# Chunk-selected attention with a LayerNorm-MLP behind it: the gain folded into W1, less work on VectorE, and a new order

## The chip, the core and the metric

One core of one Trainium2 chip runs the whole kernel in one launch. The metric is the device time in microseconds (us), lower is better. TensorE (PE in the rows) multiplies, VectorE (DVE), ScalarE (ACT) and GpSimd (POOL) work on elements, SyncE (SP) only issues DMAs, and sixteen DMA engines move the data. Each engine takes its instructions strictly in the order in which they were written for it.

## What is computed

Attention over 4 batches, 8 heads, 768 positions and 64 dimensions, in which a query sees only the 6 key chunks (of 32 keys) with the highest upper bound, then LayerNorm, a two-layer MLP and a residual sum:

```python
k_min, k_max = k_chunks.min(axis=3), k_chunks.max(axis=3)            # 24 chunks of 32 keys
ub = np.sum(np.maximum(q * k_min, q * k_max), axis=-1)               # per query and chunk
ub = np.where(causal, ub, -1e9)                                      # only chunks up to the query's own
top_chunks = np.argsort(ub, axis=-1)[..., -6:]
scores = np.where(sel & (i >= j), q @ k.T / 8, -1e9)
x = softmax(scores) @ v                                              # heads side by side: 512 wide
xn = (x - mean(x)) / np.sqrt(var(x) + 1e-6) * g_ln
out = x + np.maximum(xn @ w_ch1, 0) @ w_ch2                          # 512 -> 2048 -> 512
```

## The kernel before, in words

Two heads share the 128 partitions: a group g (0 to 15) is one pair of heads of one batch, `b, hp = divmod(g, 4)`. The 768 positions are 6 tiles of 128. Tile 0 of every batch needs no selection and is done by the functions that end in `a` (`lda`, `turna`, `smma`, `sexpa`, `valuesa`, `norma`). Batch 0's tiles 1 to 5 are loaded by tile, for four pairs at once, and turned on TensorE by the functions that end in `t` (`ldt`, `turnt`, `boundst`, `selectt`, `masktt`). Groups 4 to 15 are loaded by 32-wide blocks (`ldb`) and turned on VectorE (`turn`).

For each group: `kbound` takes minimum and maximum of a chunk's keys (DVE), `kdiag` makes the bound's operand from them (POOL), `qhi`, `qlo`, `qrel` split q into parts of 16 bits (ACT, DVE), `bounds` multiplies them (PE, into PSUM: two halves, `ub[:, :, 0]` and `ub[:, :, 1]`), `select` (DVE) adds the two halves and the causal term, finds the eight largest of each row and writes a mask, `maskt` turns it (PE), `mring` and `qring` put mask and q where the scores' matmul reads them. Then `smm` (PE), `sexp` (ACT), `diag` (POOL), `values` (PE), `norm` (DVE) give x in a range r of tiles (r=0: tiles 1 and 2, r=1: tiles 3 to 5), and `pstat` takes its statistics, one pair at a time.

A unit u is what the MLP works on at once: units 0 and 1 are the tiles 0 of batches 0, 1 and 2, 3; unit 2+2b+r is range r of batch b. `centre` (L621) subtracts the mean and multiplies by g (tile `gall`), one instruction of 512 columns per tile (L629); the result `xc` is turned either on TensorE (`xtp`, L648, copied out by `xtc`; units 0 and 1) or by a transposing DMA on SP's queue (`xt`, L642, L646; the other units). `m1` (L670) multiplies by a quarter of W1, `relu` (L686, ACT) evicts, `m2` (L699) multiplies by W2, `fin` (L708) adds x and stores. W1 and W2 come in four quarters each through POOL's queue (`w1`, `w2`), which turns them to 16 bits.

Nothing schedules this: a hand-written table of names, `ORDER`, is run from front to back, and every engine's instructions are tied to that order:

```python
for one in ORDER.split():
    what, _, way = one.partition("@")
    other[0] = int(way or 0)
    ...
    env[fn](*(int(a) if a.isdigit() else a for a in args))
    for ins in done[n:]:
        if ins.engine in queues:
            if ins.engine in ahead:
                tc.add_manual_dep(ins, ahead[ins.engine], inorder, reason="order")
```

So an instruction that waits holds up all that stands behind it on its engine, on SP's and POOL's DMA queues too. PSUM gives four one-bank buffers (`ps_t`) and two two-bank buffers (`ps_m`).

Of the kernel before, what the change touches and what calls it, by code (L numbers as in the profile page):

```python
# [850 lines left out]
```

## Time and profile before

| | |
|---|---|
| median of 3 runs | 295.56 us (294.69 to 296.43) |
| the profiled execution | 296.29 us, of which the trace's span is 294.6 us |
| PE busy | 263.3 us, 89% of the span |
| DVE busy | 217.8 us, 74% |
| ACT busy | 175.6 us, 60% |
| POOL busy | 109.3 us, 37% |
| mean granted clock of TensorE | 0.954 |
| DMA | 31.52 MB, mean 107 GB/s |

Shares of the whole span mix stages. The page's strip of 40 slices shows three of them: up to about 40 us DVE is full while PE has gaps and a lower clock, then a stretch to 220 us in which PE and DVE are both nearly full (with a hole at 66 to 74 us), then 70 us in which PE alone works without a gap. So the table says where to look for a time, and the rows of the stages say what it is worth.

### The profile page before, as it was taken

The numbers are of one execution on the slowest core, as the hardware profiler recorded it, in microseconds if no ns is written. First come the engines' busy times: TensorE is split into PE (matmuls) and PEld (weight loads), VectorE is DVE, ScalarE is ACT, GpSimd is POOL, SyncE is SP. The second block draws the span as 40 slices with busy tenths as digits, with TensorE's granted clock in tenths as the row PEclk, the third lists the DMA queues.
The fourth block names the chain that finished last, engine by engine and source line by source line (L and its number), as shares of the span: only waits on it lengthen the run. The fifth ranks groups of instructions, "written<-read, shape, count | busy, mean of one in ns | idle before, by whom it ended". The sixth has DMA issues, their size and how long they took to land.

```text
span 294.6 us, 6890 instructions
## 1 busy us (share of the span) xinstructions
PE 263.3 (89%) x2680; PEld 183.5 (62%) x2680; DVE 217.8 (74%) x627; ACT 175.6 (60%) x223; POOL 109.3 (37%) x209
## 2 busy tenths in 40 slices
PE   3658789991999997999899989998999999999995
PEld 3446679870677664666587656766776756775553
DVE  6989999733859899999999999999974238331122
ACT  2735767331489787878578867895666755343320
POOL 8783854500712327842440443445523111010000
PEclk9855799997799999999999999999999999999999
DMA  9999897198948799994889438145922102032012
GB/s 165 218 216 180 110 207 124 32 141 131 108 108 135 144 167 142 174 149 65 130 136 185 88 66 140 27 45 76 87 71 60 38 0 56 17 85 77 36 48 98
DMA packets 127601, 31.52 MB, mean 107 GB/s; under 512 B 118608, under 2 KB 124496, under 8 KB 127568
## 3 DMA queue, kind: packets, MB, share of 16 engines
q1 hardware_dynamic: 93936, 22.43, 39.3%
q0 software_dynamic: 29328, 7.34, 26.3%
q10 hardware_dynamic: 4304, 1.31, 2.4%
q8 instruction: 21, 0.34, 0.5%
q14 instruction: 12, 0.10, 0.1%
HBM read 27.53 MB, written 6.29 MB: 115 GB/s over the span
## 4 chain that ended last, share of the span: by engine, by line
PE 50%; DVE 24%; DMA 10%; SPq 8%; POOL 3%; issue 2%; ACT 2%; DVEq 0%; POOLq 0%
PE mm L670 21%; PE yp L699 17%; SPq L202 6%; PE mm L534 6%; DMA qnb<-in_q_dram 4%; PE sm L568 3%; DVE xc L629 3%; DMA knb<-in_k_dram 2%; DVE ot L708 2%; DVE qnT L405 2%; DVE m L477 1%; DVE q L418 1%; DMA out_dram<-ot 1%; DVE QB L117 1%; DVE knT L405 1%
## 5 line engine op out<-in xcount | busy, mean ns | idle before, releaser
L545 ACT ACTIVATE pt<-mm 128x1024 f16<-128x1024 f32 (+2 forms) x96 | 81.0, 880 | 29.5 <-PE mm L534 28.2
L699 PE MATMUL yp<-w2b,hT 128*128 128x512 f16 (+2 forms) x400 | 93.3, 371 | 0.3 <-DVE ot L708 0.3
L670 PE MATMUL mm<-xT,w1b 128*128 128x256 f16 (+1 forms) x640 | 90.3, 296 | 2.6 <-DMA xT<-xc 1.5
L670 PEld LDWEIGHTS <-w1b 128*128 128x128 f16 x640 | 62.2, 99 | 25.1 <-issue 2.0
L686 ACT ACTIVATE hT<-mm 128x768 f16<-128x768 f32 (+1 forms) x56 | 49.7, 900 | 44.2 <-PE mm L670 40.4
L699 PEld LDWEIGHTS <-hT 128*128 128x128 f16 x400 | 37.2, 98 | 33.4 <-DVE x L582 0.5
L553 POOL TENSOR_SCALAR_AFFINE_SELECT pt<-pt 128x512 f16<-128x512 f16 (+1 forms) x32 | 25.5, 802 | 69.7 <-ACT pt L545 69.6
L708 DVE SCALAR_TENSOR_TENSOR ot<-yp,rstd,x 128x512 f32<-128x512 f32 (+2 forms) x25 | 17.8, 718 | 29.1 <-PE yp L699 23.6
L534 PE MATMUL mm<-QA,KA 128*128 128x128 f16 (+2 forms) x224 | 34.0, 247 | 1.8 <-ACT pt L545 0.6
L534 PE MATMUL mm<-QB,KB 128*128 128x128 f16 (+2 forms) x224 | 33.8, 247 | 0.2
L568 PEld LDWEIGHTS <-pt 128*128 128x128 f16 x640 | 23.6, 98 | 4.2 <-POOL pt L553 0.5
L640 POOL TENSOR_TENSOR rstd<-ve,mhalf 128x2 f32<-128x2 f32 (+1 forms) x10 | 8.3, 828 | 47.1 <-DVE ve L637 43.4
L568 PE MATMUL sm<-va,pt 128*128 128x65 f16 x520 | 24.0, 194 | 0.5 <-ACT pt L545 0.3
L534 PEld LDWEIGHTS <-KA 128*128 128x128 f16 x224 | 18.0, 100 | 10.1 <-issue 0.8
L212 POOL DMA_DIRECT2D va<-in_v_dram x24 | 21.4, 894 | 0.7 <-issue 0.5
L534 PEld LDWEIGHTS <-KB 128*128 128x128 f16 x224 | 18.5, 101 | 4.8 <-issue 1.4
L629 DVE SCALAR_TENSOR_TENSOR xc<-x,mv,gall 128x512 f16<-128x512 f32 x24 | 19.3, 850 | 0.0
L581 DVE RECIPROCAL rden<-sm 128x4 f32<-128x4 f32 (+1 forms) x32 | 5.6, 176 | 17.9 <-PE sm L568 17.9
L619 DVE BATCH_NORM_STATS2 bst<-x 128x6 f32<-128x128 f32 x80 | 17.8, 278 | 0.1
L405 DVE STREAM_TRANSPOSE qnT<-qnb 128x640 f32<-128x640 f32 x12 | 10.0, 831 | 9.9 <-DMA qnb<-in_q_dram 9.9
L415 ACT ACTIVATE q<-qnT 128x640 f16<-128x640 f32 x12 | 8.8, 736 | 13.8 <-DVE qnT L405 13.3
L582 DVE TENSOR_TENSOR x<-sm,rden 128x256 f32<-128x256 f32 (+1 forms) x32 | 15.7, 491 | 1.1
(105 smaller groups left out, 353.8 us busy)
## 6 DMA issues: line engine op xcount, KB each, us to landing
out_dram<-ot SPq DMA_DIRECT2D x23, 256.0 KB, 2.1
qnb<-in_q_dram SPq DMA_DIRECT2D x48, 80.0 KB, 2.8
knb<-in_k_dram SPq DMA_DIRECT2D x48, 80.0 KB, 3.1
w1b<-in_moe_w_ch_dram POOLq DMA_DIRECT2D x4, 512.0 KB, 6.8
w2b<-in_moe_w_ch_dram POOLq DMA_DIRECT2D x4, 512.0 KB, 9.3
va<-in_v_dram POOLq DMA_DIRECT2D x24, 80.0 KB, 3.7
knt<-in_k_dram SPq DMA_DIRECT2D x5, 256.0 KB, 6.4
qnt<-in_q_dram SPq DMA_DIRECT2D x5, 256.0 KB, 7.1
```

The lines of the kernel that those rows point to most:

```text
L212: nc.gpsimd.dma_start(va[:, hh, :, 0:D], v[b, 2 * hp + hh, P:S].rearrange("(t p) d -> p t d", p=P))
L405: nc.vector.transpose(t, st[g][nm].rearrange("p c e -> p (c e)"))
L534: nc.tensor.matmul(sc[:, hh, o:o + w * P], ks[:, (t - 1) * P:t * P] if t else k0, qs[:, (s - 1) * P:(s - 1 + w) * P], start=True, stop=True,)
L545: nc.scalar.activation(st[g]["pt", r][:, 4 * i:4 * i + o].rearrange("p n h x -> p h n x"), st[g]["sc", r, i][:, :, 0:o * P].rearrange("p h ...
L553: nc.gpsimd.affine_select(out=dv, in_=dv, compare_op=ALU.is_ge, fill=0.0, base=0, pattern=[[0, 2 * (z - a)], [1, P]], channel_multiplier=-1,)
L568: nc.tensor.matmul(pv[:, hh, s - a, :], pt[:, where[t, s], hh, :], va0[:, b * H + 2 * hp + hh, 0:D + 1] if t == 0 else sb[t]["va"][:, 2 * ...
L619: nc.vector.bn_stats(half(u)["st"][:, i, hp], flat(xt_(u)[:, i, 2 * hp:2 * hp + 2]))
L629: nc.vector.scalar_tensor_tensor(h["xc"][:, i, :], flat(xt_(u)[:, i]), h["mv"][:, i, 0:1], gall, op0=ALU.subtract, op1=ALU.mult,)
L670: nc.tensor.matmul(hp_[:, i // (per(u) // 2), o:o + w], w1b[:, kt, (m + i) * P:(m + i + 1) * P], h["xT"][:, kt], start=(kt == 0), stop=(kt ...
L686: nc.scalar.activation(o, i, ACTF.Relu, scale=HS)
L699: nc.tensor.matmul(h["yp", i][:, cs], h["hT", kt // 4][:, kt % 4, i * P:(i + 1) * P], w2b[:, kt, cs], start=(kt == 0), stop=(kt == KT2 - 1),)
L708: nc.vector.scalar_tensor_tensor(ot[:, cs], h["yp", i][:, cs], h["rstd"][:, i:i + 1], flat(xt_(u)[:, i])[:, cs], op0=ALU.mult, op1=ALU.add,)
```

## The change

- `gall` (g over all partitions) goes; g is loaded as a column (`gcol`) and multiplied into W1 once, in place, by 16 instructions of `w1g` (DVE, 128x512 f16). `centre` only subtracts the mean, with a TENSOR_SCALAR in the place of the SCALAR_TENSOR_TENSOR.
- `lows`/`lowst` copy one half of the bounds out of PSUM on ACT. `select` then adds the two halves in one instruction for all columns, the causal term in a second one on the 4 columns of each row's own chunks alone, and `max` looks only at columns up to the own chunks.
- `pstat` takes statistics of two pairs at once: 40 instructions of 256 columns, where there were 80 of 128.
- x of unit 2 is turned on TensorE too (`xtp.2`, `xtc.2`), beside units 0 and 1.
- `zeros`, `warm.14` and `busy(n)`: products of a zero tile, 128x256 each, ahead of named PE steps, into the buffer that the step then fills: 14 at the start and 83 further ones, of which all but five stand ahead of the first `m1` in PE's order.
- A new `ORDER`.

The diff, cut to its core:

```diff
-    causf = const.tile([P, NQ, 2, NCH], F32, name="causf", tag="causf")
+    causd = const.tile([P, NC4], F32, name="causd", tag="causd")
-    gall = const.tile([P, DM], F32, name="gall", tag="gall")
+    gcol = const.tile([P, KT1], F32, name="gcol", tag="gcol")
+    zer = const.tile([P, 2 * P], F16, name="zer", tag="zer")
+    def busy(o):
+        for _ in range(other[0]):
+            nc.tensor.matmul(o, zer[:, 0:P], zer, start=True, stop=True)
...
+    def w1g(j):
+        c = slice(j * HID // 4, (j + 1) * HID // 4)
+        eng = pick(nc.vector, nc.gpsimd)
+        for kt in range(KT1):
+            eng.tensor_scalar(w1b[:, kt, c], w1b[:, kt, c], gcol[:, kt:kt + 1], None, op0=ALU.mult)
...
     def turnt(s, nm):
         ps = sb[s][nm + "T"] = ps_t.tile([P, HP, P], F32, name="tr", tag="one")
+        busy(ps[:, 0:2].rearrange("p n x -> p (n x)"))
...
+    def lows(g):
+        st[g]["ubl"] = smp.tile([P, NQ, 2, NCH], F32, name="ubl", tag="ubl", bufs=1)
+        copy(pick(nc.scalar, nc.vector), st[g]["ubl"], st[g]["ub"][:, :, 1])
     def select(g):
-        nc.vector.tensor_tensor(ubt, ub[:, :, 1], causf, ALU.add)
-        nc.vector.tensor_tensor(ubm, ub[:, :, 0], ubt, ALU.add)
+        nc.vector.tensor_tensor(ubm, ub[:, :, 0], st[g]["ubl"], ALU.add)
+        nc.vector.tensor_tensor(own, own, causd.unsqueeze(1).unsqueeze(1).to_broadcast([P, NQ, 2, NC4]), ALU.add)
         for s in range(NQ):
             for hh in range(2):
-                nc.vector.max(m8[:, s, hh, :], ubm[:, s, hh, :])
+                nc.vector.max(m8[:, s, hh, :], ubm[:, s, hh, 0:(s + 2) * NC4])
...
-            nc.vector.bn_stats(half(u)["st"][:, i, hp], flat(xt_(u)[:, i, 2 * hp:2 * hp + 2]))
+            nc.vector.bn_stats(half(u)["st"][:, i, hp // 2], flat(xt_(u)[:, i, 2 * hp - 2:2 * hp + 2]))
...
-            nc.vector.scalar_tensor_tensor(
-                h["xc"][:, i, :], flat(xt_(u)[:, i]), h["mv"][:, i, 0:1], gall, op0=ALU.subtract, op1=ALU.mult,
+            pick(nc.vector, nc.gpsimd).tensor_scalar(
+                h["xc"][:, i, :], flat(xt_(u)[:, i]), h["mv"][:, i, 0:1], None, op0=ALU.subtract,
             )
...
-        ident rows lda.0.kn masks small lda.0.qn rrows.3 turna.0.kn rrows.1 kbounda.0 ldt.1.kn ldt.2.kn ldt.1.qn
...
+        zeros warm.14 rows small ldt.1.kn ldt.2.qn ldt.2.kn ident turnt.1.kn turnt.2.qn qhit.2 lda.0.kn rows0
+        lda.0.qn turnt.2.kn@6 ldva.0 rrows.1 turna.0.kn@6 rrows.0 qlot.2 ldt.1.qn kboundt.1 kdiagt.1 kbounda.0
...
```

What the table does to the engines' queues shows at three places. The first is SP's queue behind the last loads of batch 0 (`knt`, `qnt` are its tiles, `qnb`, `knb` the blocks of groups 4 and on). Before:

```order
L219 DMA knt_754<-in_k_dram 128x8x64
L219 DMA qnt_824<-in_q_dram 128x8x64
L646 DMA_TRANSPOSE xT_922<-xc_869 128x4x128 x2
L202 DMA qnb_1024<-in_q_dram 32x20x32 x4
L202 DMA knb_1031<-in_k_dram 32x20x32 x4
```

And now:

```order
L233 DMA knt_660<-in_k_dram 128x8x64
L233 DMA qnt_1055<-in_q_dram 128x8x64
L216 DMA qnb_1082<-in_q_dram 32x20x32 x4
L216 DMA knb_1087<-in_k_dram 32x20x32 x4
L216 DMA qnb_1255<-in_q_dram 32x20x32 x4
L216 DMA knb_1381<-in_k_dram 32x20x32 x4
L216 DMA qnb_1386<-in_q_dram 32x20x32 x4
L744 DMA out_0_dram<-ot_1399 128x512
```

The two transposing DMAs of unit 2's `xc` no longer stand ahead of the first blocks.

The second is DVE around the centring of unit 0 (`bst`, `mv` are its statistics, `x2_590` and `x2_597` unit 2's x, written as groups finish). Before:

```order
L399 BN_STATS bst_500<-x2_501 128x6 x2
L627 BN_AGGR mv_624<-bst_500 128x2 x2
L629 SCALAR_TENSOR_TENSOR xc_625<-x2_501,mv_624,gall_116 128x512 x2
L581 RECIPROCAL rden_669<-sm_533 128x4
L582 TENSOR_TENSOR x2_590<-sm_533,rden_669 128x2x2x64
```

And now:

```order
L657 BN_AGGR mv_616<-bst_468 128x2 x2
L659 TENSOR_SCALAR xc_617<-x2_469,mv_616 128x512 x2
L611 RECIPROCAL rden_625<-sm_581 128x4
L612 TENSOR_TENSOR x2_597<-sm_581,rden_625 128x2x2x64
L196 TENSOR_SCALAR w1b_114<-w1b_114,gcol_116 128x512 x4
L611 RECIPROCAL rden_689<-sm_630 128x4
```

W1's first quarter is now multiplied on DVE, behind the centring of unit 0, and all that follows on DVE waits for that quarter's landing.

The third is POOL's queue, where the quarters of W1 (`w1b`) and W2 (`w2b`) are issued. Before, W1's four stood close together:

```order
L182 DMA w1b_114<-in_moe_w_ch1_dram 128x4x512
L553 AFFINE_SELECT pt0_452<-pt0_452 128x512
L374 AFFINE_SELECT pta_489<-pta_489 128x1024
L182 DMA w1b_114<-in_moe_w_ch1_dram 128x4x512 x2
L553 AFFINE_SELECT pt0_457<-pt0_457 128x512
L182 DMA w1b_114<-in_moe_w_ch1_dram 128x4x512
```

Now the last of them is issued behind the scale of unit 0 (`rstd`), and behind W2's first quarter:

```order
L279 TENSOR_TENSOR BH_110<-bdt_860,BH_110 128x4x2x4
L670 TENSOR_TENSOR rstd_872<-ve_873,mhalf_100 128x2
L190 DMA w1b_114<-in_moe_w_ch1_dram 128x4x512
L199 DMA w2b_115<-in_moe_w_ch2_dram 128x4x512
L670 TENSOR_TENSOR rstd_1051<-ve_1052,mhalf_100 128x2
```

The first quarter moved ahead, the fourth back to where POOL has waited for DVE's statistics.

## Rows read from the trace of the kernel before

**Rows 1.** Windows: stretch, length, busy PE PEld DVE ACT POOL, clock, DMA, GB/s

```profile
0.00:39.00 39.00, 24.60 (x239) 19.19 (x240) 34.69 (x83) 21.24 (x33) 27.96 (x55) 0.74 1.27 179
39.00:66.00 27.00, 26.50 (x273) 22.08 (x270) 20.41 (x69) 14.13 (x19) 10.46 (x29) 1.00 0.83 118
66.00:74.10 8.10, 1.63 (x9) 0.55 (x7) 2.65 (x14) 1.81 (x3) 0.00 (x0) 0.74 0.88 137
74.10:80.00 5.90, 5.90 (x39) 4.04 (x40) 5.56 (x11) 2.35 (x3) 4.57 (x9) 0.78 0.92 106
...
100.00:200.00 100.00, 94.94 (x1086) 65.42 (x1086) 98.03 (x294) 76.11 (x99) 43.18 (x78) 1.00 0.78 120
...
220.00:290.00 70.00, 69.97 (x567) 42.84 (x566) 23.54 (x65) 30.42 (x38) 7.53 (x10) 1.00 0.16 49
```

**Rows 2.** Waits of SP's own queue, 20 to 100 us

```profile
SPq L646 <- DVE xc L629: 29.9, 1, 29.9
```

**Rows 3.** The chain that ended last, 55 to 80 us: start, length, what

```profile
56.83 1.25 SPq L646
...
61.76 9.57 DMA qnb<-in_q_dram
...
71.35 0.85 DVE qnT L405
...
74.10 0.61 PE trh L321 x4
```

**Rows 4.** PE in order of time: start, length, instruction, count, idle before it

```profile
9.10 0.63 PE L239 MATMUL tr<-ident_f,qnt 128*128 128x128 f32 x4 [0.34 <-DMA qnt<-in_q_dram]
...
11.76 1.04 PE L239 MATMUL tr<-ident_f,qnt 128*128 128x128 f32 x4
...
38.98 1.91 PE L670 MATMUL mm<-xT,w1b 128*128 128x256 f16 x16
...
74.10 0.61 PE L321 MATMUL trh<-ident_h,MN 128*128 128x128 f16 x4 [6.47 <-DVE MN L313]
74.50 3.01 PE L670 MATMUL mm<-xT,w1b 128*128 128x256 f16 x16
```

**Rows 5.** DVE groups by form: count, busy us, mean ns, idle before

```profile
L629 DVE SCALAR_TENSOR_TENSOR xc<-x,mv,gall 128x512 f16<-128x512 f32 x24 | 19.3, 850 | 0.0
L619 DVE BATCH_NORM_STATS2 bst<-x 128x6 f32<-128x128 f32 x80 | 17.8, 278 | 0.1
...
L473 DVE TENSOR_TENSOR ubt<-ub,causf 128x240 f32<-128x240 f32 x12 | 4.7, 391 | 4.1 <-PE ub L462 4.1
...
L283 DVE SCALAR_TENSOR_TENSOR r<-q 128x512 f16<-128x512 f16 x5 | 3.4, 687 | 0.0
...
L340 DVE TENSOR_REDUCE kcs<-tr 128x16 f32<-128x512 f32 x4 | 2.7, 674 | 0.0
...
L399 DVE BATCH_NORM_STATS2 bst<-x 128x6 f32<-128x512 f32 x4 | 2.6, 680 | 0.0
...
L282 DVE TENSOR_SCALAR r<-q 128x512 f16<-128x512 f16 x5 | 1.7, 348 | 0.0
```

**Rows 6.** DVE in order of time, first 40 us

```profile
3.86 0.32 DVE L117 COPY KA<-RT 64x640 f16<-64x640 f16 x1 [1.69 <-POOL RT L134]
4.20 1.92 DVE L117 COPY KB<-RT 64x640 f16<-64x640 f16 x1
...
29.96 2.21 DVE L629 SCALAR_TENSOR_TENSOR xc<-x,mv,gall 128x512 f16<-128x512 f32 x2
```

**Rows 7.** ACT groups by form

```profile
L545 ACT ACTIVATE pt<-mm 128x256 f16<-128x256 f32 x16 | 6.1, 383 | 5.5 <-PE mm L534 5.5
```

**Rows 8.** ACT in order of time

```profile
35.03 1.02 ACT L117 COPY xT<-xq 128x1024 f16<-128x1024 f16 x1
```

**Rows 9.** DMA issues on the page, median us from issue to landing

```profile
w1b<-in_moe_w_ch_dram POOLq DMA_DIRECT2D x4, 512.0 KB, 6.8
```

**Rows 10.** DMA issues of the window 55 to 75 us

```profile
w2b<-in_moe_w_ch_dram POOLq DMA_DIRECT2D x2, 512.0 KB, 10.5
```

More of the change, by code (lines that the diff above doesn't have):

```diff
@@ L292, in boundst @@
         w = (s + 1) * NC4
+        busy(ub.rearrange("p n a h c -> p (n a h c)")[:, 0:2 * P])
         for n in range(HP):
@@ L297, in boundst, with lowst @@
                 )
+    def lowst(s):
+        w = (s + 1) * NC4
+        sb[s]["ubl"] = smp.tile([P, HP, 2, NCH], F32, name="ubl", tag="ubl", bufs=1)
+        copy(pick(nc.scalar, nc.vector), sb[s]["ubl"][:, :, :, 0:w], sb[s]["ub"][:, :, 1, :, 0:w])
     def selectt(s):
@@ L562, in values @@
         full = ps_t.tile([P, 512], F32, name="sm", tag="one")
+        busy(full[:, 0:2 * P])
         w = 2 * (z - a) * (D + 1)
@@ L602, in half @@
         if u not in hf:
-            hf[u] = dict(st=smp.tile([P, nt(u), HP, nc.vector.BN_STATS_DIM], F32, name="bst", tag=f"bst{nt(u)}"))
+            hf[u] = dict(st=smp.tile([P, nt(u), HP // 2, nc.vector.BN_STATS_DIM], F32, name="bst", tag=f"bst{nt(u)}"))
         return hf[u]
@@ new lines @@
+        m2.2.0.3 ldb.5.kn ldb.7.qn kdiag.4 sexp.1.1.0 smm.0.1.3 fin.0.0 diag.0.1 qlo.5 sexp.1.1.2 bounds.4
+        sexp.0.1.3 lows.4 qring.5 turn.5.kn ldb.8.qn smm.0.1.1 smm.0.1.2 sexp.0.1.1 qrel.5 m2.0.1.3 diag.1.1
+        select.4 smm.2.1.0 sexp.0.1.2 values.1.1 fin.2.0 smm.3.1.2 values.0.1 m2.2.1.1 kcopy.4 sexp.2.1.0
+        norm.1.1 kbound.5 maskt.4 sexp.3.1.2 smm.3.1.0 sexp.3.1.0 smm.3.1.1 ldb.8.kn ldb.6.qn sexp.3.1.1
+        m2.2.1.2 norm.0.1 kdiag.5 qring.4 fin.0.1 smm.2.1.1 sexp.2.1.1 table pstat.1.1 bounds.5 turn.7.qn
@@ new lines @@
+        m1.4.4 ldb.11.kn m1.4.0 norm.6.1 relu.4.4 m1.4.8 ldv.14 relu.4.0 ldb.12.kn maskt.9 kbound.10 fin.3.0
+        m1.4.12 pstat.7.1 kcopy.10 relu.4.8 kdiag.10 qhi.11 smm.8.1.1 m2.4.0.0 centre.5 bounds.10 mring.9
+        turn.11.kn qlo.11 relu.4.12 qring.10 sexp.8.1.1 xt.5.0 xt.5.2 smm.9.1.0 xt.5.1 smm.9.0.0 kbound.11
+        lows.10 m2.4.1.0 sexp.9.1.0 turn.12.qn sexp.9.0.0 smm.9.1.2 ldb.13.kn sexp.9.1.2 select.10 qhi.12
+        m2.4.0.1 smm.8.1.3 ldb.13.qn m2.4.0.2 ldb.14.qn kdiag.11 values.8.0 qring.11 smm.9.1.1 m2.4.1.1 diag.9.1
@@ new lines @@
+        sexp.8.1.3 m1.5.6 sexp.9.1.1 norm.8.0 qlo.12 m1.5.8 maskt.10 relu.5.6 smm.9.0.1 turn.12.kn kbound.12
+        diag.9.0 relu.5.8 fin.3.2 m2.4.1.2 sexp.9.0.1 kcopy.11 smm.9.1.3 qrel.11 m1.5.4 sexp.9.1.3 rstd.4
+        relu.5.4 kdiag.12 ldb.15.qn diag.8.1 qrel.12 bounds.11 lows.11 mring.10 smm.8.1.2 turn.13.kn m2.4.0.3
+        m2.4.1.3 sexp.8.1.2 select.11 fin.4.1 bounds.12 fin.4.0 kcopy.12 m1.5.2 smm.10.0.1 values.8.1 rstd.5
+        values.9.0 ldv.11 sexp.10.0.1 smm.10.1.3 ldb.14.kn relu.5.2 lows.12 sexp.10.1.3 turn.13.qn m1.5.0
@@ new lines @@
+        m2.5.0.0 qlo.14 smm.11.1.2 pstat.11.0 ldv.12 sexp.10.1.2 m2.5.2.2 smm.11.1.0 sexp.11.1.2 sexp.11.1.0
+        centre.6 smm.12.0.0 turn.15.qn xt.6.1 m2.5.0.1 smm.11.1.1 diag.10.1 xt.6.0 m2.5.2.3 bounds.13
+        sexp.11.1.1 turn.14.kn kbound.14 sexp.12.0.0 diag.11.1 smm.12.1.1 pstat.9.1 fin.5.2 lows.13 select.13
+        values.10.1 norm.10.1 kdiag.14 m1.6.12 kcopy.14 values.11.1 sexp.12.1.1 qrel.14 norm.11.1 qhi.15
+        relu.6.12 m1.6.0 qlo.15 turn.15.kn relu.6.0 m1.6.4 m1.6.8 relu.6.4 qring.14 maskt.13 diag.12.0
```

187 lines of the change are left out of this document (87 added, 100 removed).

## The prediction, made before the changed kernel was run

> **What bounds the kernel now.** I read the windows first, one per stage, because the shares of the whole span mix stages with different limits [rows 1]. From 220 to 290 us PE is busy 69.97 of 70 us at the full clock (2.4 GHz): whatever of PE's work stands there costs its whole length. From 100 to 200 us DVE is busy 98.03 us and PE 94.94: both are nearly full, and PE stands idle for 5.1 us. From 39 to 66 us PE is full (26.50 of 27). The first 39 us are another matter: DVE is busy 34.69 us, PE only 24.60, so PE loses 14.4 us there, and its granted clock is a mean of 0.74, that is, part of it at the lower level (1.2 GHz). From 66 to 74.1 us PE works 1.63 us and loses 6.5, and in the 5.9 us after it the clock is 0.78.
>
> The change takes almost nothing from PE: the same products must be made. So the time is PE's work plus what PE loses, and I ask of every part which loss it makes smaller: the start (14.4 us), the hole at 66 us (6.5 us), the middle (5.1 us).
>
> For the hole I read the chain and then SP's queue. The chain goes from a transposing DMA on SP (56.83 us) to the load of the first block of group 4, which takes 9.57 us and ends at 71.33; VectorE turns it, only then makes a mask that had been ready to be made, and PE, waiting for that mask, starts at 74.10 after 6.47 us of nothing [rows 3, 4]. The load was late because SP had stood for 29.9 us, in one piece, on unit 2's `xc` [rows 2].
>
> **The change, part by part.** Durations are those of the profiled execution, 296.29 us, of which 294.6 is its span; the median of the runs, 295.56, lies 0.7 us lower.
>
> *The hole.* In the new order of SP's queue the two transposes of unit 2 are gone and the blocks of group 4 stand directly behind the last tiles of batch 0. What they then wait for is a free buffer, which `turnt.3.kn` gives back; that step stands ahead of the first `m1` on PE, so the loads can be issued before 40 us, not at 58, and land before VectorE asks for them, behind the selections of tiles 3 and 5. The 6.5 us go, and with them the slow products behind the hole: 16 of them took 3.01 us at 74.50 where 16 of the same form took 1.91 at 38.98 [rows 4], so 1.1 us. Together -7.6; the bounds are 0, if something else is late there, and -8.1, the length of the whole stretch. I take nearly all of it, since the new order has products of units 0, 1 and 2 (most of their `m1` and `m2`) to fill this time. What is late next is W1's last quarter (below).
>
> *The start.* The first `m1` begins at 38.98 [rows 4]. Its chain: VectorE is full until it centres unit 0 at 29.96, for 2.21 us [rows 6]; ACT copies the turned tile at 35.03 to 36.05 [rows 8]; then PE has three us of other steps in front. The new list of VectorE up to that centring holds the same five pairs of reductions (0.67 us each [rows 5]), the same two selections, one pair of row copies and one `norm` more, about a microsecond, and POOL begins the row tile ahead of the identity, so that VectorE starts about half a microsecond sooner. Unit 0 is centred again at about 30, in less time. In PE's new order five short steps stand between its turn and `m1.0.0`, so I put the first `m1` at about 33, 6 us sooner. W1's first quarter, 6.8 us from issue to landing [rows 9], is issued near the start and does not hold it. One microsecond is lost again, since the second unit's copy stands behind other evictions on ACT: -5. Bounds: 0, if ACT's queue holds the copy as before, and -8, if PE's steps on this chain also run at the higher clock: four transposes took 0.63 us at 9.10 and 1.04 at 11.76 [rows 4], and there are some ten such steps.
>
> *Less on VectorE.* The 24 centrings took 0.85 us each [rows 5]. A TENSOR_SCALAR from f32 to 16 bits is not in the trace; from below, the one on 16 bits takes 0.348 at the same 512 columns (against 0.687 for a SCALAR_TENSOR_TENSOR on the same data), from above the old 0.85. I take 0.45, nearer to the same instruction: -9.6 us. Statistics of 256 columns lie between 0.278 (128) and 0.680 (512) [rows 5]; on the line between them 0.41, so 40 x 0.41 = 16.4 in place of 17.8: -1.4. The second sum of a selection took 0.391 on 240 columns; the new one on 40 columns is between nothing and that, I take 0.2: 12 x 0.19 = -2.3. `w1g` adds 16 x 0.348 = +5.6. In all VectorE loses 7.7 us, most of it behind 100 us, while the addition lies ahead. There PE's 5.1 us are the most that can come back; I take -3 (bounds 0 and -5), as some of these waits are for DMAs and ACT.
>
> *The copy on ACT.* Twelve `lows` of 240 columns cost about what an eviction of 256 does, 0.383 us [rows 7], and five shorter ones: 6.5 us more on ACT, which is busy 76 of 100 us in the middle [rows 1]. It is hidden there, but it stands in the chain from bounds to mask, and VectorE waits for it in order. If that cover goes, it costs 17 x 0.383 = 6.5 us. I take 0.
>
> *Zero products.* 97 of 256 columns; 16 of that width took 1.91 us, 0.12 each [rows 4]. All but five lie ahead of the first `m1`, where PE lost 14.4 us: hidden there, and if that cover is gone 97 x 0.12 = 11.6 us, or 97 x 0.19 = 18.4 at the slow rate of 74.50 [rows 4]. The five behind: +0.6.
>
> *Turning unit 2 on PE.* Eight transposes of 16 bits, 0.61 us for four at 74.10 [rows 4]: +1.2 at most, I take +0.4 at the full clock. The copy (1.02 us [rows 8]) lies on ACT.
>
> *W1's last quarter.* It is issued on POOL behind the scale of unit 0 and beside W2's quarters; VectorE then waits for it in `w1g.3`, with the selections of tiles 3 and 5 behind that. By 6.8 us [rows 9] it lands about when VectorE gets there; by the 10.5 us that W2's took [rows 10], some 3 us later. I take +1.
>
> *A port.* The second copy of the rows took 1.92 us, the first 0.32 [rows 6], while POOL copied the same tile. The Trainium skill (GPSIMD Engine Reference, Key points) says that GpSimd shares its SBUF interfaces with VectorE and contends with instructions in a two-port mode or with two SBUF inputs; the trace agrees, with this pair. The new centrings, the products with g and the own-chunk sums would be of those kinds.
>
> Sum: -7.6 - 5 - 3 + 0.6 + 0.4 + 1 = -13.6. 296.29 - 13.6 = 282.7 for a profiled execution, and 0.7 less, **282.0 us**, for the median; the cases below are medians too.
>
> **The rivals.**
>
> *More comes back (0.13).* All three losses reach their lower bounds: -8.1 - 8 - 5 + 2 = -19.1, so 276.5, and a few us less if the new order also mends the gaps outside these stretches. For it: VectorE is the fuller engine in two of the three stages. Against: every bound at once.
>
> *The port takes VectorE's gain (0.10).* Each of 57 new instructions (24 centrings, 16 products, 17 sums) meets POOL at work with the chance of its busy share in the middle, 0.43 [rows 1], and then waits at most the 1.6 us by which that copy was longer; at a third of it this is 13 us, more than the 7.7 saved. The -3 of the middle goes and some 2 of the start: 287.0. For it: the pair above. Against: the TENSOR_SCALAR group of 0.348 holds both sorts.
>
> *The hole comes back under another name (0.11).* VectorE stands in `w1g.3` until W1's last quarter has landed, and PE runs out of products again: the -7.6 becomes 0, so 289.6. For it: loads took 9.6 to 10.5 us there [rows 3, 10]. Against: the quarter is issued some 15 us earlier than those.
>
> *The zero products delay PE: slower (0.07).* They stand in PE's queue ahead of the transposes and wait for the same buffers. If they start when the buffer comes free and the data are there already, each costs its whole length on the chain of the start. At 0.19 us this is 18.4 us; taken with a start that gains nothing else, 282.0 + 5 + 17.8 = 304.8 (the 0.6 is in the sum already). It turns the sign from about 53 of the 97 on: 287.0 + 53 x 0.19 = 297.1. Against: VectorE, not PE, is full in the start.
>
> *No change (0.04).* The parts cancel: the hole and the start give back what they gain; 295.6.
>
> **How the numbers follow.** My forecast (0.55) spans 277 to 288 by the bounds of its terms. A difference of 0.5%, 1.5 us, is about what a measurement of this kernel can tell from no change. Faster by more: 0.55 + 0.13 + 0.10 + 0.11 = 0.89; same 0.04; slower 0.07. The range takes in the forecast's span, the port, the returned hole and most of the larger gain: 273.5 to 291.5.
>
> **What would show it.** First `m1` of unit 0 at about 33 us; no gap of PE over 3 us between 40 and 100; SP's queue without a 30 us wait; centrings near 0.45 us; PE idle under 3 us from 100 to 200. A first `m1` behind 37 us, a wait of VectorE for `w1b` of several us, or zero products that end later than the data they cover would prove me wrong.

## The result, and the profile after

The changed kernel takes 283.8 us (median of 4 runs, 283.73 to 284.29) where the kernel before took 295.1 (4 runs, 294.52 to 296.43): 0.961 of it, 95% interval [0.958, 0.965]. The forecast was 282.0. The trace's span fell from 294.6 to 282.0 us; parts are compared below by spans.

The page after: busy times with their share of the span, and TensorE's granted clock in 40 slices.

```profile
PE 265.9 (94%) x2785; PEld 188.2 (67%) x2785; DVE 208.5 (74%) x604; ACT 181.4 (64%) x241; POOL 110.2 (39%) x209
...
PEclk9999999999999999999999999999999999999999
```

VectorE works 9.3 us less than before, and the clock stays at its upper level from the first slice on. The windows after, with the columns of [rows 1]:

```profile
0.00:39.00 39.00, 30.23 (x348) 24.72 (x350) 33.38 (x94) 21.90 (x34) 26.87 (x53) 1.00 1.31 181
39.00:66.00 27.00, 25.17 (x255) 20.96 (x255) 20.85 (x68) 16.31 (x22) 12.84 (x32) 1.00 1.09 158
66.00:80.00 14.00, 14.00 (x123) 9.31 (x120) 12.44 (x30) 9.34 (x12) 5.86 (x11) 1.00 0.56 60
100.00:200.00 100.00, 97.76 (x1138) 70.10 (x1137) 94.86 (x265) 78.63 (x105) 49.01 (x88) 1.00 0.81 112
```

From 66 to 80 us PE works without a gap, where before it worked 1.63 + 5.90 of the same 14 us [rows 1]: the hole is gone. From 100 to 200 us PE gains 2.82 us and VectorE is 3.17 us less busy. In the first 39 us PE is busier by 5.6 us, but the zero products are counted in that. The blocks of group 4, whose late load made the hole, are now issued at 35.66 us:

```profile
35.66 4.93 SPq L216 DMA_DIRECT2D qnb<-in_q_dram  x4
```

Two of PE's rows in order of time, for [rows 4]:

```profile
35.96 1.91 PE L701 MATMUL mm<-xT,w1b 128*128 128x256 f16 x16
41.80 3.65 PE L701 MATMUL mm<-xT,w1b 128*128 128x256 f16 x32
```

The first `m1` comes at 35.96 us (38.98 before), not at the forecast 33. The second row is the pair `m1.2.0`, `m1.0.4`: unit 2's first products and more of unit 0's. It becomes the yardstick of the start below. VectorE in the first 33 us, in order of time:

```profile
4.02 1.94 DVE L122 COPY KA<-RT 64x640 f16<-64x640 f16 x1
5.97 1.93 DVE L122 COPY KB<-RT 64x640 f16<-64x640 f16 x1
...
17.52 1.01 DVE L168 MEMSET MN<- 128x320 uint32 x3
18.97 0.26 DVE L327 TENSOR_TENSOR ubm<-ub,ubl 128x96 f32<-128x96 f32 x1 [0.44 <-ACT ubl L122]
20.20 0.19 DVE L328 TENSOR_TENSOR ubm<-ubm,causd 128x32 f32<-128x32 f32 x1 [0.96 <-POOL causd L146]
...
31.82 1.01 DVE L659 TENSOR_SCALAR xc<-x,mv 128x512 f16<-128x512 f32 x2
```

And two rows of VectorE in the kernel before, beside those of [rows 6]:

```profile
0.94 1.01 DVE L160 MEMSET MN<- 128x320 uint32 x3 [0.94 <-PEq L835]
...
6.13 1.93 DVE L117 COPY KA<-RT 64x640 f16<-64x640 f16 x1
```

Unit 0 is centred at 31.82 us, 1.9 us later than before [rows 6], though the centring itself takes 1.01 us in place of 2.21. The two slow row copies are not the reason, since two were as slow before (1.92 and 1.93 us). The lists differ by one quick pair of row copies, by one `norm`, by the MEMSET of `MN`, which before was done while VectorE had nothing else to do, and by waits: 1.7 us between 3.35 and 31.82 us, where it waited 0.8 us before. The new instructions, by form:

```profile
L649 DVE BATCH_NORM_STATS2 bst<-x 128x6 f32<-128x256 f32 x40 | 14.3, 408 | 0.1
L659 DVE TENSOR_SCALAR xc<-x,mv 128x512 f16<-128x512 f32 x24 | 11.8, 541 | 0.0
...
L196 DVE TENSOR_SCALAR w1b<-w1b,gcol 128x512 f16<-128x512 f16 x16 | 5.4, 400 | 0.0
L501 DVE TENSOR_TENSOR ubm<-ub,ubl 128x240 f32<-128x240 f32 x12 | 4.7, 392 | 2.6 <-ACT ubl L122 2.6
L122 ACT COPY ubl<-ub 128x240 f32<-128x240 f32 x12 | 4.3, 359 | 0.0
...
L502 DVE TENSOR_TENSOR ubm<-ubm,causd 128x40 f32<-128x40 f32 x12 | 3.0, 251 | 0.4
```

A row's busy time is less than count times mean, since neighbouring instructions overlap. VectorE waits 2.6 us for ACT's copies in these groups and 1.7 us for those of batch 0's tiles, never for W1. The centring's mean mixes two cases. Three centrings, POOL's instruction beside them, and three centrings with POOL idle:

```profile
95.80 1.83 DVE L659 TENSOR_SCALAR xc<-x,mv 128x512 f16<-128x512 f32 x3
```

```profile
95.66 0.89 POOL L582 TENSOR_SCALAR_AFFINE_SELECT pt<-pt 128x768 f16<-128x768 f16 x1
```

```profile
148.02 1.25 DVE L659 TENSOR_SCALAR xc<-x,mv 128x512 f16<-128x512 f32 x3
```

### The profile page after: what moved, and what is told of

Its sections match the earlier page's. It is cut to its first block, busy times and chain, and to the rows that moved or that the text cites. A ratio compares the mean times of both kernels' runs of the same rounds, so it can differ in the third digit from the quotient of the medians.

```text
span 282.0 us, 7100 instructions
## 1 busy us (share of the span) xinstructions
PE 265.9 (94%) x2785; PEld 188.2 (67%) x2785; DVE 208.5 (74%) x604; ACT 181.4 (64%) x241; POOL 110.2 (39%) x209
## 4 chain that ended last, share of the span: by engine, by line
PE 75%; DVE 12%; POOL 4%; ACT 3%; issue 2%; SPq 2%; DMA 1%; DVEq 0%; POOLq 0%; ACTq 0%
PE mm L701 28%; PE yp L730 25%; PE mm L563 10%; PE sm L598 5%; PE ub L484 3%; DMA knb<-in_k_dram 1%; SPq L216 1%; PE trh L514 1%; ACT KB L122 1%; DVE bst L649 1%; DVE KA L122 1%; DVE KB L122 1%; POOL bdt L273 1%; ACT KA L122 1%; DVE kcs L260 1%
## 5 line engine op out<-in xcount | busy, mean ns | idle before, releaser
L574 ACT ACTIVATE pt<-mm 128x1024 f16<-128x1024 f32 (+2 forms) x96 | 81.9, 881 | 23.5 <-PE mm L563 22.2
L701 PEld LDWEIGHTS <-w1b 128*128 128x128 f16 x640 | 61.5, 98 | 22.4 <-issue 2.0
L563 PE MATMUL mm<-QA,KA 128*128 128x128 f16 (+2 forms) x224 | 33.2, 242 | 1.2 <-ACT pt L574 0.9
L670 POOL TENSOR_TENSOR rstd<-ve,mhalf 128x2 f32<-128x2 f32 (+1 forms) x10 | 9.3, 937 | 51.9 <-DVE ve L667 51.9
L598 PEld LDWEIGHTS <-pt 128*128 128x128 f16 x640 | 22.9, 97 | 3.3 <-issue 0.9
L563 PEld LDWEIGHTS <-KA 128*128 128x128 f16 x224 | 17.8, 98 | 10.7 <-issue 1.5
L649 DVE BATCH_NORM_STATS2 bst<-x 128x6 f32<-128x256 f32 x40 | 14.3, 408 | 0.1
L116 PEld LDWEIGHTS <-zer 128*128 128x128 f16 x83 | 7.9, 97 | 6.8 <-issue 5.2
L659 DVE TENSOR_SCALAR xc<-x,mv 128x512 f16<-128x512 f32 x24 | 11.8, 541 | 0.0
L471 POOL TENSOR_TENSOR kcs<-kcs 128x24 f32<-128x24 f32 x12 | 3.5, 292 | 20.0 <-DVE kcs L461 19.9
```

Of the source, the lines that this page charges most:

```text
L563: nc.tensor.matmul(sc[:, hh, o:o + w * P], ks[:, (t - 1) * P:t * P] if t else k0, qs[:, (s - 1) * P:(s - 1 + w) * P], start=True, stop=True,)
L574: nc.scalar.activation(st[g]["pt", r][:, 4 * i:4 * i + o].rearrange("p n h x -> p h n x"), st[g]["sc", r, i][:, :, 0:o * P].rearrange("p h ...
L598: nc.tensor.matmul(pv[:, hh, s - a, :], pt[:, where[t, s], hh, :], va0[:, b * H + 2 * hp + hh, 0:D + 1] if t == 0 else sb[t]["va"][:, 2 * ...
L649: nc.vector.bn_stats(half(u)["st"][:, i, hp // 2], flat(xt_(u)[:, i, 2 * hp - 2:2 * hp + 2]))
L659: pick(nc.vector, nc.gpsimd).tensor_scalar(h["xc"][:, i, :], flat(xt_(u)[:, i]), h["mv"][:, i, 0:1], None, op0=ALU.subtract,)
L701: nc.tensor.matmul(hp_[:, i // (per(u) // 2), o:o + w], w1b[:, kt, (m + i) * P:(m + i + 1) * P], h["xT"][:, kt], start=(kt == 0), stop=(kt ...
```

## The experiments

Ratios are to the kernel before, measured on the same chip between the runs of each group; its medians there were 296.4 (the first four runs), 296.5 (the next four), 295.3 (the next three) and 295.2 (the last).

### The hole: blocks_first

The kernel before, with two names moved in its table.

```diff
-  ... kdiagt.5 qrelt.3 xt.2.1 ... relu.1.0 ldb.4.qn turn.4.qn ldb.4.kn w2.2 ...
+  ... kdiagt.5 qrelt.3 ldb.4.qn ldb.4.kn xt.2.1 ... relu.1.0 turn.4.qn w2.2 ...
```

> The kernel before with one edit in its order: the loads of group 4's first blocks (q and k) stand ahead of the two transposing DMAs of unit 2 on SP's queue, not behind them. If SP's 29.9 us wait made the hole, VectorE no longer waits 8.7 us for the block, PE's 6.5 us before the mask go, and the time is about 7.6 us below the kernel before: 287 to 289. If the hole is due to the transfers of W2 beside it or to something else that is late there, the gain is under 3 us: 292 to 295.

Measured: 288.3 us (287.37 to 289.48), ratio 0.972 [0.967, 0.977], span 286.7. Its windows:

```profile
66.00:80.00 14.00, 14.00 (x121) 9.39 (x120) 9.06 (x18) 9.59 (x11) 6.66 (x12) 1.00 0.95 141
100.00:200.00 100.00, 95.18 (x1095) 66.67 (x1094) 98.03 (x282) 74.85 (x96) 46.35 (x85) 1.00 0.71 110
```

This edit alone takes 294.6 - 286.7 = 7.9 us from the span: the hole fills and the middle stays as it was (VectorE 98.03 us in both). The 30 us of SP's queue cost what the chain said, and this one change of order is worth most of the whole gain of 12.6 us.

### The zero products: no_zero_products

The changed kernel without `warm.14` and with every number behind an `@` taken out, so without any of the 97.

```diff
-  zeros warm.14 rows small ... turnt.2.kn@6 ... turnt.1.qn@12 ... boundst.2@11 ...
+  zeros rows small ... turnt.2.kn ... turnt.1.qn ... boundst.2 ...
```

> The changed kernel without any of the 97 zero products (neither the 14 at the start nor the 83 ahead of named steps); nothing else differs. If they only fill time in which PE waits anyway, as the prediction's sum has it, the time stays within 1.5 us of the changed kernel's 283.8, although the granted clock of the first 39 us falls to 0.7 to 0.8. If they give something by holding the clock, PE's steps on the start's chain get slower: the first m1 starts 2 to 5 us later than at 35.96 and the time is 286 to 289. If they delay PE, the time falls to 282 or less.

Measured: 284.9 us (284.44 to 285.74), ratio 0.961 [0.956, 0.965], span 282.7. The first 36 us, and then unit 2's first products:

```profile
0.00:36.00 36.00, 19.97 (x216) 15.45 (x216) 29.84 (x83) 18.91 (x31) 25.71 (x52) 0.81 1.28 179
```

```profile
42.41 3.65 PE L701 MATMUL mm<-xT,w1b 128*128 128x256 f16 x32 [0.38 <-ACT xT L122]
```

Without the products the granted clock is 0.81 in the first 36 us, against 1.00 with them, so they do lift TensorE to its upper level. The Trainium skill (TensorE: Matmul & The Clock Gate, Part 1) describes a gate that follows how busy TensorE has been; the two clocks agree with that. But unit 2's products start only 0.6 us later, and the intervals of the two ratios coincide: products and clock together show neither a cost nor a gain that these runs can tell. PE's first bounds, in the changed kernel and then without the products, show what this part of the start waited for:

```profile
17.67 0.21 PE L311 MATMUL ub<-BH,q 128*128 128x48 f16 x2 [0.20 <-POOL BH L279]
```

```profile
17.65 0.24 PE L311 MATMUL ub<-BH,q 128*128 128x48 f16 x2 [2.01 <-POOL BH L279]
```

In both they start when POOL's `BH` is there. What the lower clock alone costs is not shown, since this run takes products and clock away together.

### VectorE's shorter work in the old order: vector_part_alone, copies_at_once, old_order_no_copy

vector_part_alone is the kernel before, in its order, with g multiplied into W1, the own-chunk sum with the copy on ACT, and statistics over two pairs. Each `w1g` stands just ahead of the first `m1` that needs it, each copy just ahead of its selection.

```diff
+  ... w1g.2 m1.0.8 ... w1g.0 m1.0.0 ... w1g.1 m1.1.4 ... w1g.3 m1.1.12 ...
-  ... bounds.4 turn.5.kn sexp.0.1.3 ... values.1.1 select.4 ...
+  ... bounds.4 turn.5.kn sexp.0.1.3 ... values.1.1 lows.4 select.4 ...
```

> The kernel before, in its own order, with the three changes to VectorE's work alone: g multiplied into W1 (each quarter just ahead of the first m1 that reads it), the causal term on own chunks alone with one half of the bounds copied by ACT, statistics over two pairs. If what VectorE saves comes back in the middle, PE's idle time from 100 to 200 us falls from 5.1 to about 2 and the time is 290 to 293. If the gain needs the new order, since each engine goes on in the old one, the time is within 1.5 us of the kernel before. If the products of W1 or the copies on ACT hold up the start, it is 1 to 4 us slower.

Measured: 312.4 us (311.30 to 315.35), ratio 1.052 [1.046, 1.058], span 313.7 (of the longest execution): every expectation missed, VectorE has less to do and the kernel is 16 us slower. VectorE's largest wait of the new kind, then one instance on VectorE and what ACT did meanwhile:

```profile
DVE ubm L491 <- ACT ubl L117: 25.1, 11, 5.4
```

```profile
111.06 0.41 DVE L491 TENSOR_TENSOR ubm<-ub,ubl 128x240 f32<-128x240 f32 x1 [5.41 <-ACT ubl L117]
```

```profile
108.35 0.81 ACT L563 ACTIVATE pt<-mm 128x768 f16<-128x768 f32 x1 [1.52 <-PE mm L552]
109.18 0.73 ACT L117 CAST KA<-knT 64x640 f16<-64x640 f32 x1
109.92 0.72 ACT L117 CAST KB<-knT 64x640 f16<-64x640 f32 x1
110.67 0.36 ACT L117 COPY ubl<-ub 128x240 f32<-128x240 f32 x1
```

PE's bounds were done at 104.35 us. The copy takes 0.36 us, but it stands in ACT's queue behind an exponential that waits for PE, and behind two casts; VectorE stands still for 5.41 us. So the next run moved only the copies:

```diff
-  ... bounds.4 turn.5.kn sexp.0.1.3 ... values.1.1 lows.4 select.4 ...
+  ... bounds.4 lows.4 turn.5.kn sexp.0.1.3 ... values.1.1 select.4 ...
```

> The run vector_part_alone (before's order with the shorter VectorE work, 312.4 us) with one thing moved: each copy of a half of the bounds stands directly behind its bounds in the order, not directly ahead of its selection. Theory A, the copy stood behind exponentials on ACT, and VectorE waited for that: the 29 us of VectorE's waits for the copy shrink to under 8, and the time falls to 293 to 299 us, the kernel before less what shorter VectorE work is worth in it. Theory B, the loss is from the products of W1 with g, which make VectorE wait for W1 in the old order, and the waits for the copy only sit on top: the time stays above 307 us. Theory C, ACT has no room for the copies in the old order wherever they stand: 301 to 307 us, with the waits moved to other ACT results.

Measured: 303.0 us (301.33 to 303.57), ratio 1.022 [1.017, 1.028], span 300.8. VectorE's wait, and two windows:

```profile
DVE ubm L491 <- ACT ubl L117: 6.3, 4, 2.8
```

```profile
39.00:66.00 27.00, 22.10 (x200) 17.54 (x201) 20.12 (x74) 11.84 (x17) 10.13 (x29) 0.94 0.60 88
...
100.00:200.00 100.00, 95.28 (x1079) 65.44 (x1077) 92.95 (x265) 79.25 (x107) 43.94 (x79) 1.00 0.78 120
```

The place of the copies was worth 9.4 us: their waits fell from 25.1 to 6.3 us, and PE from 100 to 200 us went from 88.46 to 95.28. But the time lies in the range of theory C, not in that of theory A: some 6.5 us remained over the kernel before. A part of theory C is in the trace, since PE's waits for ACT's exponentials rose from 1.5 to 4.1 us. From 39 to 66 us PE works 4.4 us less than before [rows 1], which this run alone does not tell between the copies and W1's products. The third run leaves the selection as it was:

```diff
-    def lows(g):
-        copy(pick(nc.scalar, nc.vector), st[g]["ubl"], st[g]["ub"][:, :, 1])
...
+        nc.vector.tensor_tensor(ubt, ub[:, :, 1], causf, ALU.add)
+        nc.vector.tensor_tensor(ubm, ub[:, :, 0], ubt, ALU.add)
```

> The kernel before with g multiplied into W1 (each quarter's products just ahead of the first m1 that uses it) and statistics over two pairs; selection and order as before, so no copy on ACT. It settles what is left of vector_part_alone (312.4 us) once copies_at_once had taken 9.4 us of it away (303.0 us). Theory A, the rest is also from the copies: the time is that of the kernel before less 0 to 3 us, 293 to 296. Theory B, the rest is from W1's products, for which PE waited 8 us between 39 and 66 us in copies_at_once: 298 to 302 us, with PE again under 24 us of the 27 there (26.50 before).

Measured: 295.0 us (10 runs, 292.38 to 296.67), ratio 0.9995 [0.996, 1.003], span 293.3. By time theory A holds: without the copies and the new selection another 8.0 us came back (303.0 to 295.0). But its windows show gains and losses that cancel:

```profile
39.00:66.00 27.00, 23.55 (x220) 18.34 (x218) 20.47 (x74) 12.42 (x18) 9.88 (x29) 0.90 0.57 82
...
100.00:200.00 100.00, 97.84 (x1149) 68.27 (x1148) 96.45 (x282) 79.29 (x102) 45.04 (x80) 1.00 0.81 125
```

In the middle PE gains 2.9 us from the shorter centrings and statistics, as in the changed kernel; from 39 to 66 us it loses 2.95 us, as theory B had it, since PE waits for the products of W1 with g there (2.9 us in its waits, `PE mm <- DVE w1b`). These two are not the whole sum: PE wins back 2.2 us from 66 to 80 us (9.69 us in place of 7.53), and over the span it is busy 2.4 us longer than before (265.8 us), at a granted clock of 0.90 from 39 to 66 us in place of 1.00. The span falls by 1.3 us, and the medians are the same. So in this order the shorter work on VectorE brings nothing that can be measured; the new order puts what is added (`w1g`, copies) where PE does not wait for it.

### Pieces undone: changed_again, old_centring, old_selection

The changed kernel was run once more beside two versions with one piece undone each.

> The changed kernel once more, beside the three runs that undo or add a piece. Every theory expects the time measured for it before, 283 to 285 us; the other runs of this group are compared with it.

Measured: 283.8 us (283.71 to 284.96), ratio 0.959 [0.956, 0.963], span 282.0.

old_centring:

```diff
-            pick(nc.vector, nc.gpsimd).tensor_scalar(
-                h["xc"][:, i, :], flat(xt_(u)[:, i]), h["mv"][:, i, 0:1], None, op0=ALU.subtract,
+            nc.vector.scalar_tensor_tensor(
+                h["xc"][:, i, :], flat(xt_(u)[:, i]), h["mv"][:, i, 0:1], gall, op0=ALU.subtract, op1=ALU.mult,
...
-  ... w1g.0 ... w1g.1 ... w1g.2 ... w1g.3 ...
```

> The changed kernel with the old centring (subtract the mean and multiply by g, 850 ns each before) and without the 16 products of W1 with g. VectorE gets 24 x 0.31 = 7.4 us more and 5.4 less; behind 100 us it is 18 to 20 centrings, about 6 us more. Theory A, shorter centrings give the middle its 2.8 us: PE idles about 5 us from 100 to 200 again, 286 to 288 us. Theory B, the new order gives the middle its 2.8 us and VectorE's length is only part of it: PE's idle time stays under 3.5 us, 283.5 to 285 us. Theory C, the products with g cost time where they stand, ahead of the first m1: the first m1 comes 1 to 2 us sooner and the time is 282 to 283 us.

Measured: 287.4 us (286.93 to 287.55), ratio 0.970 [0.967, 0.973], span 285.8. Its middle, and unit 2's first products:

```profile
100.00:200.00 100.00, 95.50 (x1101) 67.75 (x1100) 96.17 (x264) 77.80 (x105) 48.84 (x88) 1.00 0.80 115
```

```profile
42.91 3.65 PE L696 MATMUL mm<-xT,w1b 128*128 128x256 f16 x32
```

Theory A: PE stands idle 4.50 us of the 100 again (2.24 with the new centring). Of the 3.8 us of span, 1.1 are lost ahead of unit 2's products and 2.7 behind them. (With `gall` back, g is again a load of 256 KB in place of 2 KB; what that alone does was not tried.)

old_selection:

```diff
-        nc.vector.tensor_tensor(ubm, ub[:, :, 0], st[g]["ubl"], ALU.add)
-        nc.vector.tensor_tensor(own, own, causd.unsqueeze(1).unsqueeze(1).to_broadcast([P, NQ, 2, NC4]), ALU.add)
+        nc.vector.tensor_tensor(ubt, ub[:, :, 1], causf, ALU.add)
+        nc.vector.tensor_tensor(ubm, ub[:, :, 0], ubt, ALU.add)
```

> The changed kernel with the old selection: both sums over all columns on VectorE, maxima over all columns, no copy on ACT. Theory A, the copy is hidden by its place in the order: VectorE gets 12 x (0.391 - 0.251) = 1.7 us more in the sums and something more in the maxima, and the time rises by 0 to 2 us, to 284 to 286. Theory B, VectorE's waits for the copy (2.6 us in the changed kernel) are on the path: they go, and the time falls to 281 to 283.

Measured: 285.4 us (284.92 to 286.88), ratio 0.965 [0.960, 0.969], span 283.2. It lies in theory A's range, 1.6 us above the changed kernel, though the two intervals overlap; theory B's 281 to 283 is out. The copies in their new places cost nothing that undoing them would give back.

### The start: rows_later, q_loads_on_sp, centre_sooner, first_m1_sooner

rows_later is the changed kernel with a pair of row copies moved away from POOL's, and POOL's causal constant made sooner, ahead of W1's first issue.

```diff
-  ... turna.0.kn@6 rrows.0 qlot.2 ... ldva.1 lda.1.kn rrows.3 ... kdiagt.2 ldvt.1 ... lowst.2 caus qringt.1 ...
+  ... turna.0.kn@6 qlot.2 ... ldva.1 lda.1.kn rrows.0 rrows.3 ... kdiagt.2 caus ldvt.1 ... lowst.2 qringt.1 ...
```

> The changed kernel with two edits in its order: the second pair of row copies on VectorE (which took 1.9 us each beside GpSimd's copies of the same rows) moves behind the first bounds, and the causal constant is made ahead of W1's first load on GpSimd's queue, not behind it (VectorE waited 1.0 us for it). If the start is bound by VectorE, the first m1 starts 2 to 4 us sooner than at 35.96 and the time is 280 to 282. If ACT, GpSimd's bounds or the loads bound it, it stays within 1 us of 283.8.

Measured: 282.8 us (282.21 to 284.04), ratio 0.954 [0.949, 0.959], span 282.3 (of the longest execution). The copies that took 1.9 us now take 0.32, yet unit 0 is centred at 31.93 and the first `m1` is at 36.35: the 3.3 us that VectorE no longer works in the first 39 us, it now waits. The longest of these waits stands where the copies stood. VectorE, ACT, and the issues on ACT's queue (ns: shortest, median, longest):

```profile
6.69 0.69 DVE L291 SCALAR_TENSOR_TENSOR q<-tr,q 128x512 f16<-128x512 f32 x1 [2.68 <-ACT q L288]
```

```profile
6.06 0.60 ACT L288 ACTIVATE q<-tr 128x512 f16<-128x512 f32 x1 [3.98 <-PE tr L254]
...
10.72 3.62 ACTq L206 DMA_DIRECT2D rawa<-in_q_dram  x2
14.39 0.60 ACT L288 ACTIVATE q<-tr 128x512 f16<-128x512 f32 x1 [3.41 <-DMA rawa<-in_k_dram]
```

```profile
L206 ACTq DMA_DIRECT2D rawa<-in_q_dram x4: 374/400/1032, 6.1 to 14.5; - x4
```

VectorE waits 2.68 us for the first q, which ACT can copy only when PE has turned the first tile of q. The 3.62 us on ACT's queue are not the work of issuing: the row runs from the start of one issue to the end of the next, and none of the four took over 1.03 us. In between ACT stands still, and its next row names the landing of a load of k as what ended the wait; VectorE then waits 0.39 us for the second q. The next run moves such issues to SP's queue, on the reading that issuing held ACT.

```diff
-  ... lda.1.qn ... lda.3.qn ... lda.2.qn ...
+  ... lda.1.qn@1 ... lda.3.qn@1 ... lda.2.qn@1 ...
```

> On top of rows_later (282.8 us, first m1 at 36.35): three loads of q, tiles 0 of batches 1, 3 and 2, are issued on SP's queue, not on ACT's. In rows_later two of these issues held ACT from 10.72 to 14.34 us, and VectorE waited for ACT's q. Theory A, the blocked ACT holds the start: VectorE's waits for ACT's q fall from 7.5 to under 5 us, the first m1 comes at 34 to 35.5, and the time is 281 to 282. Theory B, the loads themselves hold the start (the DMA engines' share is about 1.0 over the first 36 us): the waits reappear on PE at the transposes of those q tiles, the first m1 stays at 36 to 37, and the time is 282.3 to 284.

Measured: 282.9 us (282.84 to 282.99), ratio 0.959 [0.954, 0.964], span 281.3. The first `m1` at 35.18 is in theory A's range, the time in theory B's. Theory A's wait does not fall: ahead of the centring VectorE waits 3.0 us for ACT's q, after 3.1 in rows_later (of the 7.5 us in the expectation 4.4 lie at about 62 us, in both). Still the centring starts at 30.48, 1.45 us sooner. Rows of rows_later, in order of time, and the clock of its 16 to 18 us:

```profile
15.77 2.50 PE L116 MATMUL ub<-zer 128*128 128x256 f16 x11 [0.97 <-DVE q L291]
18.07 0.28 PE L311 MATMUL ub<-BH,q 128*128 128x48 f16 x2
...
22.00 0.65 PE L355 MATMUL tr<-ident_f,rawa 128*128 128x128 f32 x4 [1.36 <-DMA rawa<-in_q_dram]
```

```profile
16.00:18.00 2.00, 2.00 (x11) 1.40 (x10) 1.94 (x6) 1.80 (x4) 1.79 (x7) 0.50 1.67 193
```

And the first bounds of q_loads_on_sp:

```profile
17.13 0.21 PE L311 MATMUL ub<-BH,q 128*128 128x48 f16 x2 [1.52 <-POOL BH L279]
```

About half of the 1.45 us goes with the moved issues: in rows_later PE waited 1.36 us for a tile of q that came late, and VectorE 0.86 us at 27.20 for PE's products behind it, and q_loads_on_sp has neither wait. The other half is there at the first bounds, where the traces differ in the clock: in rows_later PE had worked 1.4 of the 4 us from 12 to 16, the granted clock was 0.50 (the lower level) from 16 to 18 us, and 11 zero products took 2.50 us, where they took 1.36 in the changed kernel. POOL's `BH` was done at 17.25, so in that execution, the longest of its four, the zero products held the bounds up by 0.8 us. Whether the moved issues kept the clock up in q_loads_on_sp is not shown, and the medians of the two runs differ by 0.1 us.

centre_sooner puts unit 0 ahead of two pairs of reductions (`kbounda.1`, `kbounda.3`), on top of rows_later:

```diff
-  ... pstata.1 kcopya.3 ... kbounda.1 ... kbounda.3 norm.3.0 ... centre.0 ... xtp.0 w1g.0 ... smma.3 xtc.0 ... m1.0.0 ...
+  ... pstata.1 centre.0 kcopya.3 ... w1g.0 kbounda.1 ... xtp.0 values.0.0 kbounda.3 norm.3.0 xtc.0 ... m1.0.0 smma.3 ...
```

> On top of rows_later: unit 0 is centred directly behind its statistics, with W1's first quarter behind it, ahead of two pairs of reductions (2.4 us); its turn, its copy and the first m1 stand sooner too. Theory A, the first m1 was late because of what stands ahead of the centring in VectorE's order: centring at about 29, the first m1 at 33 to 34, and the time 280 to 281.5. Theory B, VectorE then waits for the landing of W1's first quarter, and the reductions and all behind them are late: the first m1 at 35 or later and the time 283 to 286. Theory C, the first m1 comes sooner by 2 us or more, but what it overtakes on PE and VectorE is needed as much: 282 to 284.

Measured: 287.5 us (287.26 to 288.98), ratio 0.976 [0.971, 0.980], span 285.6. On VectorE, in order of time:

```profile
27.74 1.15 DVE L659 TENSOR_SCALAR xc<-x,mv 128x512 f16<-128x512 f32 x2
31.00 1.86 DVE L196 TENSOR_SCALAR w1b<-w1b,gcol 128x512 f16<-128x512 f16 x4 [2.10 <-DMA gcol<-in_moe_g_ln_dram]
```

The centring is 4 us sooner, and then VectorE stands waiting, not for W1 but for the 2 KB of g, which were issued at 24.74 us; all behind it is late. It is theory B with another load, and the time lies above all three ranges. The last run, on top of q_loads_on_sp, mends that: g is loaded near the start, and `w1g.0` stands behind the reductions.

```diff
-  ... rrows.1 ... gain ... pstata.1 kcopya.3 ... kbounda.3 norm.3.0 ... centre.0 ... xtp.0 w1g.0 ... smma.3 xtc.0 ... m1.0.0 ...
+  ... gain rrows.1 ... pstata.1 centre.0 kcopya.3 ... xtp.0 values.0.0 kbounda.3 w1g.0 norm.3.0 xtc.0 ... m1.0.0 smma.3 ...
```

> On top of q_loads_on_sp (282.9 us, centring at 30.48, first m1 at 35.18): the column of g is loaded near the start, unit 0 is centred ahead of two pairs of reductions, its turn and its copy stand ahead of the next exponentials, W1's first quarter is multiplied behind the reductions (not ahead of them, as in centre_sooner), and the first m1 stands ahead of two short steps. No VectorE wait for the column of g is expected, and the first m1 at 32.5 to 34. Theory A, an earlier first m1 is worth its own length: 280 to 281.8 us. Theory B, up to the first m1 PE's idle time only changes its place, because unit 0's products displace steps that others wait for: the first m1 comes 1 us or more sooner, and the time stays at 282 to 284. Theory C, as in centre_sooner, moving these steps delays unit 2 and the copies: over 284.

Measured: 285.0 us (284.68 to 286.0), ratio 0.964 [0.960, 0.968], span 283.4. PE, then VectorE, in order of time:

```profile
34.05 1.91 PE L701 MATMUL mm<-xT,w1b 128*128 128x256 f16 x16
```

```profile
36.74 0.18 DVE L611 RECIPROCAL rden<-sm 128x4 f32<-128x4 f32 x1 [2.03 <-PE sm L598]
```

The first `m1` is 1.1 us sooner than in q_loads_on_sp, and the kernel 2 us slower: theory C. Unit 0's 16 products take 1.91 us on PE ahead of the last `values` of unit 2's x; VectorE waits 2.03 us for these, and unit 2 is centred at 38.85 in place of 36.59. This shows what the start is measured by. Over all runs that differ from the changed kernel in the start alone:

| run | pair with unit 2's first products at | span | difference |
|---|---|---|---|
| q_loads_on_sp | 41.05 | 281.3 | 240.25 |
| changed kernel | 41.80 | 282.0 | 240.20 |
| rows_later | 42.11 | 282.3 | 240.19 |
| no_zero_products | 42.41 | 282.7 | 240.29 |
| first_m1_sooner | 43.20 | 283.4 | 240.20 |
| centre_sooner | 45.37 | 285.6 | 240.23 |

From that pair on, all six take the same 240.2 us to within 0.1; the first `m1` (34.05 to 36.65 us) does not order them. rows_later and q_loads_on_sp have the lowest medians, 282.8 and 282.9, but their intervals overlap that of the changed kernel, and they ran on other chips: that one of them beats it is not shown.

## Why the prediction came out as it did

The forecast, -13.6 us, stands against -12.6 measured in spans and -11.3 in medians. The hole and the middle came as forecast; that the rest of the sum is so near is in part luck, since errors in the start and in the additions are of opposite sign. Point by point:

- **The hole: right, mechanism and size.** Forecast -7.6; the order of SP's queue alone gave -7.9. The blocks are issued at 35.66 us, before the 40 us that the prediction named, and PE's longest wait from 39 to 100 us is 0.9 us.
- **The middle: right in size, by terms that were mis-sized against each other.** Forecast -3; PE gained 2.82 us. The step "I take 0.45" for the centring was too low for the mean: it measured 541 ns, 19.3 - 11.8 = 7.5 us saved in busy time where 9.6 stood. With POOL idle it fits (three in 1.25 us); what lifts the mean is instructions beside POOL's, the neighbour that the port rival named (three in 1.83 us). The statistics gave 17.8 - 14.3 = 3.5 where 1.4 stood, because the working held a count times a mean (16.4) against a row's busy time (17.8), in which overlaps are left out. The own-chunk sum measured 251 ns for the 200 taken, `w1g` 5.4 us for 5.6. In all VectorE is busy 9.3 us less, where 7.7 stood. With the old centring back, PE's idle time in the middle returns (4.50 us), so the new centring is what carries this term.
- **The start: mis-sized, and its step failed.** Forecast -5 by a first `m1` at about 33; it came at 35.96. The step that failed is "Unit 0 is centred again at about 30", read off VectorE's list alone: it came at 31.82. The list was a MEMSET of 1.01 us longer than counted, and it was taken to run without new waits, while VectorE waited 0.96 us for POOL's `causd` and 0.44 for ACT's copy. Nor is a shorter list enough: rows_later took 3.3 us out of it, and VectorE waited instead, 2.68 us of it for the first q, behind PE's first turns. And the mark itself was the wrong one, as first_m1_sooner shows: what counts is when unit 2's products begin.
- **The additions (+2): too dear.** VectorE never waited for W1's last quarter, for which +1 stood, and taking the zero products out brought nothing. What is left of the span, by difference, is -12.6 + 7.9 + 2.8 = -1.9 for the start and the additions together, where -5 + 2 = -3 stood: two errors of opposite sign.
- **The copy on ACT at nothing: right in this order, but its price without cover was far too small.** "17 x 0.383 = 6.5 us" counts the copies' own length. In vector_part_alone, what a copy waits behind on ACT counted: 9.4 us came back by moving the copies alone, and 8.0 more by leaving them and the new selection out.
- **The rivals.** The port lengthened single instructions, before the change as after it, but did not take VectorE's gain: the middle's term came. The copies beside POOL's agree with the Trainium skill (GPSIMD Engine Reference, Key points), by which GpSimd shares its SBUF interfaces with VectorE and contends with VectorE's instructions in a two-port mode or with two SBUF inputs. The hole did not return as a wait for W1. Slower by zero products fell with no_zero_products, although in rows_later's trace 11 of them do delay PE, by 0.8 us; slower did occur, by 16 us, in vector_part_alone, through a mechanism that no rival named.
